# Turning two of the first four blocks by DMA and pairing the first loads in a four-layer attention and ReGLU kernel

## The chip, the cores and the metric

One NeuronCore of a Trainium2 chip. The metric is the device time of one execution in microseconds (us), taken on several executions; medians and ranges are quoted. Each run also carries the mean clock granted to TensorE (1.000 is full). Names: PE is TensorE, DVE is VectorE, ACT is ScalarE, SP is the SyncE queue that issues most DMAs. A second DMA queue is issued from ACT. PSUM holds the results of matmuls until another engine has read them. A DMA "lands" when its completion is signalled.

## The reference, cut to what matters

```python
x = x + A(layernorm(x), wqkv, wo)            # linear attention, 32 heads of 32
x = x + B(layernorm(x), Wg, Wu, Wd)          # (relu(x Wg) * (x Wu)) Wd
x = x + A(...)                               # the same two layers once more
x = x + B(...)
# in A:  q, k, v = x @ wqkv;  phi(t) = where(t > 0, t + 1, exp(t)) + 1e-6
```

x has 2048 rows of 1024, all inputs are bf16. The 2048 rows are 16 blocks of 128; four blocks are a "quarter". A matmul needs the normalized rows transposed, so every block must be "turned".

## The kernel before

The change and the argument touch the first 60 us alone: loads of x and of the weights, LayerNorm of the first blocks, and quarter 0 of layer 0. x0 to x15 are the blocks of x; k0, k1 and q0, q1 are the weights of the first and the last 512 columns of the keys and the queries, v0 the first of the values. A *unit* is one 128x512 tile of keys or queries: eight matmuls. `norm(n)` computes the LayerNorm statistics of block n and `scale(n)` applies them; what the *join* is stands in the code. Cuts are marked.

```python
zero = self.ep.tile([P, NW], BF16, tag="e")          # idle matmuls, to warm the PE clock
nc.vector.memset(zero, 0.0)
idle = self.ps3.tile([P, NW], F32, tag="b")
for _ in range(10):
    nc.tensor.matmul(idle, lhsT=zero[:, 0:P], rhs=zero, start=True, stop=True)
k0, k1, v0, q0, q1 = (ring.place() for _ in range(5))
self.load_x(0, 0, nc.scalar)       # first half of block 0, on ACT's queue
self.load_x(0, 1)                  # second half, on SP's
self.load_x(1, None, nc.scalar)
k0(0, H)                           # weights of the keys' first 512 columns, first half
self.load_x(2, None, nc.scalar)
k0(H, 2 * H)
self.load_x(3, None, nc.scalar)
k1(); q0()
self.load_x(4); ... ; self.load_x(7)
q1()
for t in range(8, self.ST): self.load_x(t)
v0()
...
def block(j, c, n):                # scale block n, turn it on PE, copy it out of PSUM on ACT
    scale(n)
    t0 = turn(n, 0); t1 = turn(n, 1)
    t0("s"); t1("s")
    if n + 1 < QT: norm(n + 1)
    k(j, c)
return [block0, block1, lambda: k(0, 1), lambda: block(1, 1, 2), lambda: k(2, 0),
        lambda: block(2, 1, 3), lambda: k(3, 0), lambda: k(3, 1)]      # then eight query units
...
def phi(self, ps, out, kind):      # ACT makes e; DVE's "join" reads PSUM and frees it
    ...
    def join():
        if kind == "v":            # keys: e = min(e, 1) + 1e-6
            nc.vector.tensor_scalar(out=e, in0=e, scalar1=1.0, scalar2=1e-6, ...)
        nc.vector.scalar_tensor_tensor(out=out, in0=ps, scalar=0.0, in1=e,
                                       op0=ALU.max, op1=ALU.add)
    if self.phi_lag: self.later.at(self.phi_lag, join)   # 3 units later in quarter 0
...
for i in range(QT, self.ST):       # LayerNorm of blocks 4 to 15, one every 3 units from unit 8
    self.ln_at((8 if l == 0 else 2) + 3 * (i - QT), l, i, 2)
```

Projections rotate through four PSUM buffers, so a unit cannot start before the join of the unit four places earlier has ended. In quarter 0 the order of instructions on DVE and ACT is the program's.

## Time and profile before

| | us |
|---|---|
| median of the first three runs (range) | 1629.38 (1629.17 to 1629.80) |
| the run whose trace was at hand for the prediction | 1630.68, span 1628.9 |
| PE busy in that trace | 1621.7 |
| PE idle before 11.56 us | 4.0 |
| second half of k0 lands | 10.19 |

A second trace of this unchanged kernel, taken in the experiments (a run of 1629.20 us), has this in its chain of waits (start, duration, what):

```profile
1.66 7.06 DMA t<-in_A_wqkv_dram
8.71 0.04 issue
8.76 0.59 PE ps L404 x2
```

The same load of k0, issued at the same 1.66 us, lands at 8.71 us in place of 10.19, and PE runs on 1.5 us sooner. The spans of the two traces are 1627.4 and 1628.9. On average over the first 8.7 us, the later trace moves 275 GB/s, 2.39 MB in all, and the first 261 GB/s, 2.27 MB. At the 360 GB/s that both reach, the difference is worth a third of a microsecond, so most of the 1.5 us seems to lie in which bytes came first, not in how many. All 41 later runs of this kernel fall into two groups with a gap between: 25 from 1629.12 to 1629.60, the other 16 from 1630.21 up. Two traces, one from each group, are all that ties the groups to this landing; and seven of the 16, but none of the 25, have a mean clock below 1.000, so the clock may have a part in it.

### The profile page before, as it was taken

What the parts mean: (1) busy time and instruction counts of PE and PEld (TensorE: products, weight loads), DVE (VectorE), ACT (ScalarE), POOL (GpSimd) and SP (SyncE); (2) the same over time, 40 slices, a digit from 0 to 9 for tenths busy, and PEclk for the clock granted to TensorE, in tenths of its full rate; (3) what the DMA queues carried; (4) which work ended last, traced back from release to release, by engine and by line L of the source; (5) the groups of instructions that cost most, each with busy time, mean ns of one, the idle gap of its engine ahead of it and who ended that gap; (6) DMA issues with size and microseconds to landing.
All of it is one profiled execution on the core that took longest, in us unless ns stands there. A gap on an engine that the chain in (4) does not pass through costs nothing.

```text
span 1628.9 us, 18772 instructions
## 1 busy us (share of the span) xinstructions
PE 1621.7 (100%) x7754; PEld 739.3 (45%) x7754; DVE 566.7 (35%) x940; ACT 331.8 (20%) x638; POOL 201.9 (12%) x134
## 2 busy tenths in 40 slices
PE   8999999999999999999999999999999999999999
PEld 4444444444444444444444444444444444444444
DVE  7845695213212222212165547942022111111211
ACT  5741212101110110111066312121011101101110
POOL 2349220000000000000023592100000000000000
DMA  7312647448445444544560147464554454454452
GB/s 245 65 52 56 178 71 206 144 148 232 155 143 190 160 151 161 168 147 137 168 128 1 53 93 250 85 193 146 182 165 152 155 184 155 145 166 154 155 162 71
DMA packets 298246, 235.06 MB, mean 144 GB/s; under 512 B 101296, under 2 KB 294192, under 8 KB 298160
## 3 DMA queue, kind: packets, MB, share of 16 engines
q1 hardware_dynamic: 292832, 228.75, 47.7%
q10 hardware_dynamic: 5328, 5.11, 0.9%
q8 instruction: 60, 0.98, 0.3%
q14 instruction: 26, 0.21, 0.0%
HBM read 201.33 MB, written 8.39 MB: 129 GB/s over the span
## 4 chain that ended last, share of the span: by engine, by line
PE 98%; ACT 1%; DVE 1%; DMA 1%; issue 0%; SPq 0%; DVEq 0%
PE pu L639 24%; PE pg L639 24%; PE acc L663 23%; PE ps L404 12%; PE ps L530 7%; PE ps L439 7%; DMA t<-in_A_wqkv_dram 1%; PE kv L452 0%; PE acc_last L663 0%; ACT e L351 0%; ACT e L350 0%; PE fold L515 0%; DVE st L138 0%; ACT e L352 0%; DVE slab L358 0%
## 5 line engine op out<-in xcount | busy, mean ns | idle before, releaser
L639 PEld LDWEIGHTS <-t 128*128 128x128 bf16 x3584 | 350.3, 98 | 423.2
L639 PE MATMUL pu<-xnT,t 128*128 128x512 bf16 x1792 | 423.5, 379 | 0.0
L639 PE MATMUL pg<-xnT,t 128*128 128x512 bf16 x1792 | 423.4, 379 | 0.0
L663 PE MATMUL acc<-t,hT 128*128 128x512 bf16 x1764 | 382.5, 379 | 0.0
L645 DVE TENSOR_TENSOR hT<-pu,rg 128x512 bf16<-128x512 f32 x224 | 154.7, 691 | 572.0 <-PE pu L639 572.0
L644 ACT ACTIVATE rg<-pg 128x512 f32<-128x512 f32 x224 | 133.5, 596 | 737.3 <-PE pg L639 737.0
L663 PEld LDWEIGHTS <-hT 128*128 128x128 bf16 x1820 | 177.9, 98 | 209.1
L404 PE MATMUL ps<-t,xnT 128*128 128x512 bf16 x1024 | 224.3, 380 | 2.2 <-DMA t<-in_A_wqkv_dram 1.7
L404 PEld LDWEIGHTS <-xnT 128*128 128x128 bf16 x1024 | 99.2, 98 | 122.3 <-issue 4.3
L530 PE MATMUL ps<-T,pqT 128*128 128x512 bf16 x512 | 111.2, 379 | 0.0
L145 ACT ACTIVATE rstd<-mv,eps 128x1 f32<-128x1 f32 x64 | 18.7, 293 | 334.1 <-DVE mv L143 333.9
L680 DVE TENSOR_TENSOR xo<-x,acc 128x512 bf16<-128x512 f32 x31 | 21.3, 688 | 170.3 <-PE acc L663 170.3
L483 POOL TENSOR_TENSOR prod<-pq,zrow 128x1024 f32<-128x1024 bf16 x32 | 67.9, 2122 | 85.9 <-DVE den L488 72.5
L138 DVE BATCH_NORM_STATS2 stats<-x 128x6 f32<-128x512 f32 (+1 forms) x120 | 78.0, 673 | 0.8
L530 PEld LDWEIGHTS <-pqT 128*128 128x128 bf16 x512 | 49.9, 98 | 60.4 <-issue 0.5
L419 POOL CAST ksum<-x 128x512 f32<-128x512 bf16 x2 | 1.7, 866 | 605.4 <-DVE x L358 605.4
L677 DVE TENSOR_TENSOR x<-x,acc 128x512 f32<-128x512 f32 x32 | 21.6, 675 | 138.5 <-PE acc L663 137.4
L421 POOL TENSOR_TENSOR ksum<-ksum,slab 128x512 f32<-128x512 f32 x46 | 54.0, 1183 | 84.6 <-DVE slab L358 75.1
L358 DVE SCALAR_TENSOR_TENSOR pq<-ps,e 128x512 bf16<-128x512 f32 x64 | 44.0, 688 | 53.9 <-ACT e L352 52.2
L495 POOL TENSOR_TENSOR pq<-pq,den 128x1024 bf16<-128x1024 bf16 x32 | 61.7, 1933 | 3.1 <-DVE den L490 3.1
L488 DVE TENSOR_REDUCE den<-prod 128x32 f32<-128x1024 f32 x32 | 39.0, 1217 | 53.9 <-POOL prod L483 53.9
L439 PE MATMUL ps<-slab,x 128*128 128x512 bf16 x256 | 56.6, 379 | 0.0
(57 smaller groups left out, 596.0 us busy)
## 6 DMA issues: line engine op xcount, KB each, us to landing
t<-in_B_W_gate_dram SPq DMA_DIRECT2D x56, 1024.0 KB, 7.1
t<-in_B_W_up_dram SPq DMA_DIRECT2D x56, 1024.0 KB, 5.4
t<-in_B_W_down_dram SPq DMA_DIRECT2D x64, 896.0 KB, 5.2
t<-in_A_wqkv_dram SPq DMA_DIRECT2D x11, 1024.0 KB, 5.6
t<-in_A_wo_dram SPq DMA_DIRECT2D x4, 1024.0 KB, 7.2
away<-x SPq DMA_DIRECT2D x8, 512.0 KB, 4.4
x<-away SPq DMA_DIRECT2D x8, 512.0 KB, 8.5
out_dram<-xo ACTq DMA_DIRECT2D x31, 128.0 KB, 2.5
```

Of the source, the lines that this page charges most:

```text
L138: self.nc.vector.bn_stats(out=stats[:, c, :], in_=src[:, c * fmax:(c + 1) * fmax])
L358: nc.vector.scalar_tensor_tensor(out=out, in0=ps, scalar=0.0, in1=e, op0=ALU.max, op1=ALU.add)
L404: nc.tensor.matmul(by_row(ps), lhsT=self.xnT[l, l_q][:, kt, j * P:(j + 1) * P], rhs=w[:, kt, :].rearrange("p (b i d) -> p i b d", i=R, d=H ...
L421: nc.gpsimd.tensor_tensor(out=ksum[:, cols], in0=ksum[:, cols], in1=pk, op=ALU.add)
L439: nc.tensor.matmul(ps, lhsT=self.xn[l, t][:, d * P:(d + 1) * P], rhs=self.pk[l, t][:, h * NW:(h + 1) * NW], start=(t == 0), stop=(t == sel ...
L483: nc.gpsimd.tensor_tensor(out=prod, in0=pq_of[sc, j], in1=zrow, op=ALU.mult)
L495: nc.gpsimd.tensor_tensor(out=heads(pq), in0=heads(pq), in1=den[:, :].unsqueeze(2).to_broadcast([P, D // HD, HD]), op=ALU.mult)
L530: nc.tensor.matmul(ps, lhsT=pqT[sc][:, g, j * P:(j + 1) * P], rhs=T[g // 2][:, g % 2, n2 * NW:(n2 + 1) * NW], start=(g == 0), stop=(g == G ...
L639: nc.tensor.matmul(ps, lhsT=w[:, kt, fi * P:(fi + 1) * P], rhs=self.xnT[l, q][:, kt, :], start=(kt == 0), stop=(kt == KT - 1))
L644: nc.scalar.activation(out=rg, in_=pg, func=ACT.Relu)
L645: nc.vector.tensor_tensor(out=h[:, fi, :], in0=pu, in1=rg, op=ALU.mult)
L663: nc.tensor.matmul(ps[:, 0:n], lhsT=hT[ft // 4][:, ft % 4, j * P:(j + 1) * P], rhs=wd[:, k, i * n:(i + 1) * n], start=(ft == 0), stop=(ft ...
```

## The change

Blocks 2 and 3 are turned by DMA transposes in place of PE transposes, and query units are put among the key units to give those transposes time. The first loads go out in pairs, one on each queue; x4 and later are issued behind the transposes. Two more idle matmuls.

```diff
-        for _ in range(10):
+        for _ in range(12):
...
-        self.load_x(0, 0, nc.scalar)
-        self.load_x(0, 1)
-        self.load_x(1, None, nc.scalar)
-        k0(0, H)
-        self.load_x(2, None, nc.scalar)
-        k0(H, 2 * H)
-        self.load_x(3, None, nc.scalar)
-        k1()
-        q0()
-        (x4 to x7, q1, x8 to x15, v0, all on SP's queue)
+        self.load_x(0, None, act)
+        self.load_x(1)
+        k0(H, 2 * H, act)
+        k0(0, H)
+        self.load_x(2, None, act)
+        k1()
+        q0(0, 2 * H, act)
+        self.load_x(3)
+
+        def load():
+            for t in range(4, 8):
+                self.load_x(t)
+            q1()
+            for t in range(8, self.ST):
+                self.later.at(3 + (t - 8) // 2 * 2, lambda t=t: self.load_x(t))
+            self.later.at(11, v0)
...
-        def block(j, c, n): ...
+        def turned(n):
+            scale(n)
+            self.ln_turn(0, n, xn[n])              # DMA transpose
+        return ([block0, block1, lambda: (turned(2), norm(3), k(0, 1)),
+                 lambda: (turned(3), load(), k(1, 1)), lambda: q(0, 0), lambda: q(1, 0)]
+                + [lambda f=f, j=j, c=c: f(j, c) for j in (2, 3) for f, c in ((k, 0), (k, 1), (q, 0))]
+                + [lambda j=j: q(j, 1) for j in range(QT)])
...                                                # SP too now keeps the program's order
```

More of the change, by code (lines that the diff above doesn't have):

```diff
@@ L34, in place @@
         self.loaded += 1
-        return lambda lo=0, hi=8: self.nc.sync.dma_start(out=t[:, lo:hi, :], in_=src[:, lo:hi, :])
+        return lambda lo=0, hi=8, queue=None: (queue or self.nc.sync).dma_start(
+            out=t[:, lo:hi, :], in_=src[:, lo:hi, :])
     def load_to(self, n):
@@ L218, in head @@
         idle = self.ps3.tile([P, NW], F32, tag="b")
-        for _ in range(10):
+        for _ in range(12):
             nc.tensor.matmul(idle, lhsT=zero[:, 0:P], rhs=zero, start=True, stop=True)
         k0, k1, v0, q0, q1 = (ring.place() for _ in range(5))
-        self.load_x(0, 0, nc.scalar)
-        self.load_x(0, 1)
-        self.load_x(1, None, nc.scalar)
+        act = nc.scalar
+        self.load_x(0, None, act)
+        self.load_x(1)
+        k0(H, 2 * H, act)
         k0(0, H)
-        self.load_x(2, None, nc.scalar)
-        k0(H, 2 * H)
-        self.load_x(3, None, nc.scalar)
-        k1()
-        q0()
-        self.load_x(4)
-        self.load_x(5)
-        self.load_x(6)
-        self.load_x(7)
-        q1()
-        for t in range(8, self.ST):
-            self.load_x(t)
-        v0()
+        self.load_x(2, None, act)
+        k1()
+        q0(0, 2 * H, act)
[7 more added lines that the diff above has]
+            self.later.at(11, v0)
         src = self.xb
@@ L269, in turn, with head_units @@
             return take
-        return stat, rstd, scale, turn
-    def head_units(self, k, stat, rstd, scale, turn):
+        return load, xn, stat, rstd, scale, turn
+    def head_units(self, k, q, load, xn, stat, rstd, scale, turn):
         def block0():
@@ L305, in norm @@
             rstd(j)
-        def block(j, c, n):
+        def turned(n):
             scale(n)
-            t0 = turn(n, 0)
-            t1 = turn(n, 1)
-            t0("s")
-            t1("s")
-            if n + 1 < QT:
-                norm(n + 1)
-            k(j, c)
-        return [block0, block1, lambda: k(0, 1), lambda: block(1, 1, 2), lambda: k(2, 0),
-                lambda: block(2, 1, 3), lambda: k(3, 0), lambda: k(3, 1)]
+            self.ln_turn(0, n, xn[n])
[3 more added lines that the diff above has]
+                + [lambda j=j: q(j, 1) for j in range(QT)])
     def ln_turn(self, layer, t, xn):
@@ L562, in layer_A @@
         if l == 0:
-            first = self.head_units(lambda *a: k_unit(0, *a), *steps)
+            first = self.head_units(lambda *a: k_unit(0, *a), lambda *a: q_unit(0, *a), *steps)
         else:
@@ L569, in quarter0 @@
             run(first)
-            run(column_major(q_unit, 0))
-            later.at(1, lambda: None)
             self.phi_lag = 0
         if l == 0:
-            with self.tc.manual_schedule(engines={mybir.EngineType.DVE,
+            with self.tc.manual_schedule(engines={mybir.EngineType.DVE, mybir.EngineType.SP,
                                                   mybir.EngineType.Activation}):
```

## The prediction

> **What bounds the kernel now.** I read the page first: its busy times and its chain of waits.
>
> ```profile
> PE 1621.7 (100%) x7754; PEld 739.3 (45%) x7754; DVE 566.7 (35%) x940; ACT 331.8 (20%) x638; POOL 201.9 (12%) x134
> ...
> PE 98%; ACT 1%; DVE 1%; DMA 1%; issue 0%; SPq 0%; DVEq 0%
> ```
>
> TensorE (PE) is busy for 1621.7 of 1628.9 us, so all idle time together is 7.2 us, under half a percent. The change touches only the loads, the first LayerNorms and the first quarter of layer 0. A comparison of the two instruction streams per engine says the same: past this first stretch they are equal in order. So the question is at which microsecond PE leaves the first quarter. Busy time by stretch shows where PE is idle:
>
> ```profile
> core 0: us, PE busy (x) PEld busy (x) DVE busy (x) ACT busy (x) POOL busy (x), PEclk, DMA share, GB/s
> 0.00:11.56 11.56, 7.54 (x34) 3.02 (x35) 5.54 (x16) 2.92 (x7) 0.70 (x6) 1.00 0.85 285
> 11.56:19.90 8.34, 8.26 (x52) 3.96 (x50) 7.85 (x16) 4.75 (x12) 2.80 (x3) 1.00 1.08 362
> 19.90:38.90 19.00, 19.00 (x90) 8.61 (x88) 15.66 (x31) 14.72 (x29) 5.79 (x5) 1.00 0.69 194
> 38.90:60.00 21.10, 20.98 (x97) 9.34 (x96) 20.81 (x43) 16.68 (x41) 5.11 (x5) 1.00 0.46 75
> ```
>
> PE loses 4.0 us before 11.56, and 0.08, 0.00 and 0.12 us in the next three rows. The other 3 us lie in the tail, which is untouched. From 11.56 us on the DMA share is above 1 (362 GB/s): the DMA engines are full while PE works. VectorE (DVE) is nearly full in the row before PE's first transposes of block 3 and again after 38.9.
>
> The chain in order of time says what ends the 4 us and what paces the start (start, duration, what; lines left out):
>
> ```profile
> 1.66 8.53 DMA t<-in_A_wqkv_dram
> ...
> 10.23 0.59 PE ps L404 x2
> ...
> 14.98 1.28 DVE L138 BATCH_NORM_STATS2 st<-x 128x6 f32<-128x512 bf16 x2
> 16.30 0.21 DVE L143 BATCH_NORM_AGGREGATE mv<-st 128x2 f32<-128x12 f32 x1
> 16.42 0.37 DVE L356 TENSOR_SCALAR e<-e 128x512 f32<-128x512 f32 x1
> 16.90 0.69 DVE L358 SCALAR_TENSOR_TENSOR slab<-ps,e 128x512 bf16<-128x512 f32 x1
> ...
> 15.13 0.61 PE L260 MATMUL tp<-ident,x 128*128 128x128 bf16 x8
> 15.58 3.62 PE L404 MATMUL ps<-t,xnT 128*128 128x512 bf16 x16
> 19.28 0.62 PE L260 MATMUL tp<-ident,x 128*128 128x128 bf16 x8
> 19.90 6.92 PE ps L404 x32
> ```
>
> (The first two and the last line are of the chain; the others of the timeline, where a DVE or a PE line begins with its start and duration.) The second half of weight k0 lands at 10.19 us and starts PE for good. Then 32 matmuls take 6.92 us: 0.216 us each, 1.73 us for a unit of eight.
>
> **What the Trainium skill says.** "DMA: Bandwidth & Descriptors", section "Issuing engines are not separate DMA queues": loads from several issuing engines run on the same 16 DMA engines, and a second queue saves only issue time. The trace agrees: 346 GB/s from 5 to 10 us with two queues at work, 366 from 15 to 20 with one; an issue costs 0.4 to 0.5 us. So pairing changes the order of landing, not the total. "TensorE: Matmul & The Clock Gate", section "Part 4: PE-mode transpose", gives about 275 ns for a PE transpose in one kernel's context. Here eight start at 15.13 and the next matmul starts at 15.58, so one costs 56 ns of PE; the measurement decides. Same page, section "What's actually happening": the array needs about 3.4 us of sustained work to reach full clock. The trace agrees: ten idle matmuls take 4.45 us, twice the later 216 ns each. No page told me how long one DMA transpose takes; the trace does, 3.0 to 4.1 us from issue to landing for 128x1024.
>
> **The change part by part.**
>
> *PE transposes.* Sixteen go (blocks 2 and 3). By the timeline, 11.56 to 19.74 us holds 32 matmuls (6.90 us) and sixteen transposes: 8.18 us, so transposes with their small waits cost 1.28 us (0.90 of it the transposes). Saved if nothing takes their place: 1.3 us. ScalarE loses four PSUM copies of 0.54 us, off the path. Two more idle matmuls fill the wait for x0; they end at about 6.6 us and cost nothing.
>
> *The start.* Time to landing, issue by issue, before: x0 3.6 and 3.75 us, x1 5.2, k0 first half 5.7, x2 9.3, k0 second half 10.2, x3 10.5, k1 13.4, q0 16.4. Now x0 and x1 come side by side, then the two halves of k0, 1.5 MB in all. The DMA moved that many bytes by 6.9 us, and landings trail bytes moved by 1 to 2 us, so k0 is there at about 8.4 instead of 10.2. x0 comes about 0.7 us later than before, which puts the first real matmul at 8.2 to 8.4. Idle time saved: about 1.7 us at best.
>
> *What is now late: k1.* It shares the queues with x2 and then q0. At equal shares it ends when 3.7 MB are through: about 15. If q0 gets little until k1 is done, 12.8. PE wants it at 8.4 plus two units, 3.9 us with block 1's transposes, so 12.3. A wait of 0.5 to 2.8 us.
>
> *What is now late: x3.* It moves from the third x load on ScalarE's queue (landed 10.5) to behind k1 on SP's. The first 4.2 MB (x0 to x3, k0, k1, q0) are the same set of bytes in both kernels; before, the last landed at 16.4. Now x3 and q0 end that set, so x3 lands at about 15.5 to 16.4, at the earliest 14 if SP's queue gets the larger share.
>
> *And DVE waits for it in order.* In the changed program's DVE order the statistics of x3 stand ahead of the first join of the keys (lines "e" and "slab" above). There are four PSUM buffers, so the fifth unit, q(0,0), cannot start before that join ends. From the rows above: statistics 1.28, aggregate 0.21, join 0.37 + 0.69, with gaps 2.61 us (14.98 to 17.59 in the old trace). So q(0,0) starts at x3 plus 2.6: 18.1 to 19.0, 16.8 with the early x3 (there k1 at 13.3 and two units set it too).
>
> *The balance.* After q(0,0) starts, twelve units remain, 20.7 us, without PE transposes. The old kernel has eleven units after 19.90, so it ends the quarter at 38.9 and stood twelve units from the end at 18.2. The change is then 18.1 - 18.2 = -0.1 to 19.0 - 18.2 = +0.8 us, -1.4 in the best case. The gain of 1.7 + 1.3 us at the start is thus eaten by one load. The later waits: keys and queries are mixed in the second half, so ScalarE (a query takes 0.58 + 0.63 + 0.72 us, more than PE's 1.73 with the gaps) falls less behind than with eight queries in a row. The 0.12 us of PE idle near 44 us may go, but DVE enters 38.9 to 60, where it was busy for 20.81 of 21.10, with up to 1 us more backlog. I count -0.1 to +0.5.
>
> *DMA transposes.* Block 2's is wanted at about 22 (q(0,0) plus two units), issued at about 13.3 and behind x3 in the queue: lands by 18 or 19. Block 3's is issued at about 19.5, lands by 23.5, wanted at about 27. Both hidden. x4 can only be issued after it, about 20.5, and lands at about 23; q1 at about 28, wanted at about 32. Hidden too.
>
> **Rivals.** (1) *The start's gain stays.* If pairing equal loads keeps the 16 DMA engines even (landings trailed bytes by 2 us only once two unequal streams had mixed), x3 lands at 14 to 15 and the kernel gains 1 to 1.5 us: 1628. For it: k1 and q0 need only the same bytes. Against it: no view shows that pairing evens them. (2) *x3 at the end of the set holds DVE and PE*: 1629.3 to 1630.5, my main line. For it: the program's order and the equal set of bytes. (3) *Mixed queues trail further*: landings slip from 2 to 3 or 4 us behind, x3 at 17.5, and the late x4 to x7 push the normalizations into the full DVE stretch: 1631 to 1632. Against it: the trail stayed at 2 us once established. (4) *PE is the bound, all is hidden anyway* and only the transposes count: 1628. Against it: PE is not busy in the start, loads set it.
>
> **Range and chances.** Main line +0.2, with some weight on the first rival because the two queues look arranged to be even, gives 1629.4 us against 1629.38. Best case -1.5, worst about +2: the range is 1627.8 to 1631.2. Two per cent is 33 us, over four times all of PE's idle time, and a loss of that size would need a stall that nothing in the order suggests. Same: 0.98.
>
> **What would show it.** Right: first matmul of layer 0 before 9 us; in the waits, PE waiting for k1 near 12 to 15 and for DVE's join before the fifth unit; DVE idle for 2 to 3 us until x3; no PE wait on a DMA transpose; PE leaving the quarter within 1 us of the old time. Wrong: x3 landing before 14, with PE continuous from 9 us (gain of 2 us or more), or waits on transposes, x4 to x7 or q1, or new PE idle time between 40 and 60 us (loss).

## The result, and the profile after

| | runs | median us | range |
|---|---|---|---|
| before | 4 | 1629.30 | 1629.17 to 1629.80 |
| changed | 4 | 1631.49 | 1629.61 to 1632.99 |

A ratio here is the mean time of one kernel's runs over that of the other's of the same rounds, so not quite the ratio of the medians. It is 1.0012, 95% interval 0.9995 to 1.003: the same at two per cent, as forecast, but the median lies 0.3 us above my range. The spread is new too: four runs cover 3.4 us. In order, with their clocks: 1629.61 (1.000), 1631.14 (0.999), 1632.99 (0.998), 1631.85 (0.999). The trace at hand is of the first, the fastest. Its busy times by stretch, in the windows used before:

```profile
0.00:11.56 11.56, 9.23 (x41) 3.83 (x42) 6.33 (x18) 3.47 (x7) 0.70 (x6) 1.00 0.87 284
11.56:19.90 8.34, 7.50 (x35) 3.05 (x33) 6.95 (x15) 3.67 (x9) 1.84 (x2) 1.00 0.71 175
19.90:38.90 19.00, 19.00 (x90) 8.63 (x89) 18.14 (x34) 15.21 (x32) 4.71 (x5) 1.00 1.08 297
38.90:60.00 21.10, 20.91 (x98) 9.41 (x97) 21.10 (x45) 16.91 (x40) 8.27 (x7) 1.00 0.43 82
```

The columns are stretch, length, busy time of PE, PE weight loads, DVE, ACT, POOL, granted clock, DMA share and GB/s. PE is busy for 1.7 us more before 11.56, half of which (0.85) is the two idle matmuls, and for 0.8 less in the next row. The DMA share fell from 1.08 to 0.71 there: x4, issued at 5.75 us before, is now issued at 18.52, behind the transposes. DVE is full in the last row. PE's own timeline and its list of waits name the losses:

```profile
1.34 5.30 PE L221 MATMUL idle<-zero 128*128 128x512 bf16 x12 [1.34 <-DVE zero L218]
7.26 0.72 PE L262 MATMUL tp<-ident,x 128*128 128x128 bf16 x8 [0.62 <-DVE x L155]
8.35 1.47 PE L402 MATMUL ps<-t,xnT 128*128 128x512 bf16 x6 [0.37 <-ACT xnT L269]
...
10.56 1.90 PE L402 MATMUL ps<-t,xnT 128*128 128x512 bf16 x8
13.13 7.13 PE L402 MATMUL ps<-t,xnT 128*128 128x512 bf16 x30 [0.67 <-DMA t<-in_A_wqkv_dram]
```

x0 landed at 4.6 us, so the first real matmul came at 8.35, and k1 landed at 13.09, after PE had run dry. The third wait is the forecast one on DVE's order. On DVE and on PE's weight loads:

```profile
14.21 1.28 DVE L139 BATCH_NORM_STATS2 st<-x 128x6 f32<-128x512 bf16 x2 [0.47 <-DMA x<-in_A_x_dram]
15.53 0.21 DVE L144 BATCH_NORM_AGGREGATE mv<-st 128x2 f32<-128x12 f32 x1
15.66 0.37 DVE L354 TENSOR_SCALAR e<-e 128x512 f32<-128x512 f32 x1
...
16.07 0.69 DVE L356 SCALAR_TENSOR_TENSOR slab<-ps,e 128x512 bf16<-128x512 f32 x1
...
16.81 1.62 PEld L402 LDWEIGHTS <-xnT 128*128 128x128 bf16 x9 [0.56 <-DVE slab L356]
```

DVE idles for 0.47 us until x3 lands at 14.19, does its statistics, then the first join, and the fifth unit starts at 16.81: x3 plus 2.6 us, as worked out beforehand. No wait on a DMA transpose appears anywhere. From the first matmul of layer B on (237.47 us here, 238.48 in the first trace before) the two traces take 1390.36 and 1390.42 us to the end, so all of the difference lies ahead of that.

### The profile page after: what moved, and what is told of

Same layout as the page of the kernel before. It is cut to its first block, busy times and chain, and to the rows that moved or that the text cites. A ratio compares the mean times of both kernels' runs of the same rounds, so it can differ in the third digit from the quotient of the medians.

```text
span 1627.8 us, 18743 instructions
## 1 busy us (share of the span) xinstructions
PE 1621.6 (100%) x7740; PEld 739.5 (45%) x7740; DVE 567.6 (35%) x940; ACT 330.5 (20%) x634; POOL 202.0 (12%) x134
## 4 chain that ended last, share of the span: by engine, by line
PE 98%; DMA 1%; DVE 1%; issue 0%; SPq 0%; DVEq 0%
PE pu L635 24%; PE pg L635 24%; PE acc L659 23%; PE ps L402 13%; PE ps L528 7%; PE ps L437 7%; DMA x<-in_A_x_dram 1%; PE kv L450 0%; PE acc_last L659 0%; PE fold L513 0%; DVE slab L356 0%; DVE stats L139 0%; DVE e L354 0%; DVE st L139 0%; DVE pq L356 0%
## 5 line engine op out<-in xcount | busy, mean ns | idle before, releaser
L419 POOL TENSOR_TENSOR ksum<-ksum,slab 128x512 f32<-128x512 f32 x46 | 54.1, 1183 | 81.4 <-DVE slab L356 64.1
L486 DVE TENSOR_REDUCE den<-prod 128x32 f32<-128x1024 f32 x32 | 38.9, 1217 | 54.0 <-POOL prod L481 54.0
```

What stands on the lines that cost most here:

```text
L419: nc.gpsimd.tensor_tensor(out=ksum[:, cols], in0=ksum[:, cols], in1=pk, op=ALU.add)
```

## The experiments

Fourteen runs, each with five rounds. "Half" counts the runs whose mean clock was below 1.000.

| label | what | median us (range) | half |
|---|---|---|---|
| e1 | before, unchanged | 1629.39 (1629.20 to 1632.28) | 1 of 5 |
| e2 | changed, unchanged | 1630.29 (1630.17 to 1631.59) | 1 of 5 |
| e3 | changed, 10 idle matmuls | 1631.15 (1630.82 to 1632.59) | 5 of 5 |
| e4 | changed, 16 idle matmuls | 1630.71 (1629.80 to 1630.99) | 0 of 5 |
| e5 | changed, x0 in halves | 1631.01 (1630.29 to 1631.68) | 2 of 5 |
| e6 | changed, join first | 1631.43 (1630.36 to 1632.73) | 3 of 5 |
| e7 | old first loads, DMA transposes | 1628.92 (1628.71 to 1629.27) | 0 of 5 |
| e8 | new loads, PE transposes | 1631.97 (1630.54 to 1632.57) | 4 of 5 |
| e9 | e7 with join first | 1629.85 (1629.34 to 1630.10) | 0 of 5 |
| e10 | e9, LayerNorm 1 unit later | 1629.02 (1628.73 to 1629.09) | 0 of 5 |
| e11 | e4 with join first | 1630.55 (1630.46 to 1631.22) | 0 of 5 |
| e12 | e7, LayerNorm 1 unit later | 1628.90 (1628.87 to 1629.48) | 0 of 5 |
| e13 | e7, LayerNorm 2 units later | 1628.38 (1628.33 to 1628.53) | 0 of 5 |
| e14 | e4, LayerNorm 1 unit later | 1630.22 (1629.93 to 1630.43) | 0 of 5 |

The kernel before, in the same rounds: median 1630.21 beside e1 to e4, 1629.59 beside e5 to e8, 1629.47 beside e9 to e11, 1629.41 beside e12 to e14, nine runs each. Every interval of a ratio contains 1, and all results were correct. The four groups (e1 to e4, e5 to e8, e9 to e11, e12 to e14) ran on four chips. The fastest run of the kernel before was 1629.12, 1629.25, 1629.12 and 1629.19 on them, so I compare across groups, but only differences well over 0.1 us.

Not all forecasts below came in. Inside a range that was named are the medians of e3, e11 and e12 (its less hopeful case); e10 and e14 missed theirs by 0.02 us. Outside all that was named lie e4 (0.7 us above, though its clocks came as forecast), e7 (0.3 above), e9 (0.75 above), e13 (0.5 faster than e12, forecast was the same or a loss), and e5, whose three runs at full clock have a median of 1630.84. e6 and e8 are spoiled by the clock.

### Clock or noise: e1 to e4

e1 and e2 are the two kernels again. e3 and e4 change one number of the changed kernel:

```diff
-        for _ in range(12):
+        for _ in range(10):      # e3;  range(16) in e4
```

> The kernel before, unchanged, for a second trace. Theory A (the changed kernel's runs differ by how long the TensorE clock stays at half rate): every run of the kernel before has a mean granted clock of 1.000 and lies within 1629.0 to 1630.7; the profiled run of 1630.68 differs from 1629.3 by a later landing of the second half of k0 (10.2 us there, about 9 here). Theory B (chip or run noise): this one spreads over 2 us or more as the changed kernel does.

> The changed kernel, unchanged, for more draws and another trace. Theory A: times in steps of about 1.7 us (one activity window of 3.4 us at half rate costs half of it): 1629.6, 1631.3, 1633.0, each with mean clock 1.000, 0.999, 0.998. Theory B: no link of time to clock.

> The changed kernel with 10 idle matmuls as before in place of 12. If fewer idle matmuls leave PE less busy in the first microseconds, half rate lasts longer or comes more often: median 1631 to 1633. If the count does not matter (the gaps for k1 and the join do), the same spread as the changed kernel.

> The changed kernel with 16 idle matmuls: they end at 7.3 us or, cold, at 8.2, which fills the gap before the transposes of block 0. Theory A with the warm-up as cause: all runs at clock 1.000, median 1629.5 to 1630. If half rate comes from the later gaps (0.7 us for k1, 0.2 us for the join), the spread of 1629.6 to 1633 stays.

With nine runs of the changed kernel in hand (four at first, five in e2): five at full clock, 1629.61 to 1630.35; four below it, 1631.14 to 1632.99. The means differ by 1.75 us. e3 is below full clock in all five runs, e4 in none. The trace of e3 shows how it comes about (columns as above; the clock comes last but two):

```profile
1.34:4.50 3.16, 3.15 (x8) 1.20 (x9) 0.00 (x0) 0.68 (x1) 0.00 (x0) 1.00 0.80 185
4.50:7.90 3.40, 0.72 (x4) 0.10 (x1) 2.04 (x4) 0.47 (x2) 0.00 (x0) 1.00 1.08 370
7.90:11.33 3.43, 2.64 (x12) 1.34 (x13) 2.69 (x8) 1.02 (x4) 0.00 (x0) 0.50 1.09 355
11.33:14.74 3.41, 3.41 (x15) 1.73 (x14) 0.95 (x3) 0.60 (x1) 0.00 (x0) 0.50 0.93 308
14.74:18.15 3.41, 3.41 (x17) 1.56 (x16) 2.78 (x6) 0.98 (x3) 0.00 (x0) 1.00 0.07 25
```

PE's timeline of the same run has the gap (in brackets: idle before, and who ended it):

```profile
8.43 1.04 PE L262 MATMUL tp<-ident,x 128*128 128x128 bf16 x8 [3.21 <-DVE x L155]
9.73 2.74 PE L402 MATMUL ps<-t,xnT 128*128 128x512 bf16 x6 [0.26 <-ACT xnT L269]
```

The clock records of this trace begin at 4.50 us, and PEclk reads 1.00 where there is no record. The idle matmuls tell what it was before: they start 0.43 us apart until 4.50 and 0.22 us apart after it, so the clock came up there. Then PE stood for 3.21 us, until the late x0 was normalized: 0.72 us busy in 3.40. From 7.92 to 14.74 us the granted clock is 0.50, and the real matmuls that fall into this stretch take twice as long: six end after 2.74 us where the changed kernel's first trace has 1.47. The Trainium skill says in "TensorE: Matmul & The Clock Gate", section "What's actually happening", that the clock's state follows the activity in free-running windows of 3413 ns; the clock records agree. From 4.50 to 7.92 it is one such length and from 7.92 to 14.74 two; in e5, e6 and e8 the half-rate stretch is one, 3.41 us. Where the window lies differs from run to run: with idle matmuls that all start at 1.34 us, the clock comes up at 4.04 us in e6, 6.69 in the changed kernel's first trace and 7.29 in that of e2. What PE does in the 3.41 us after that is what tells the traces apart: 0.72 to 1.38 us of work in the four that then fall to half rate (e3, e6, e8, e5), 1.94 to 2.75 us in the eight others that have clock records. That is an agreement of twelve traces, and only the count of idle matmuls was varied on purpose.

So Theory A held for the changed kernel, where every run below full clock is slower than every run at it, and Theory B fell there. e1 was a miss for Theory A: it spread over 3.1 us, the very sign named for B. Its longest run, though, is again one of low clock (1632.28 at 0.998): the kernel before can lose its clock too (7 of 41 in all), only less often. e4 removes the half-rate runs but not the loss: with the clock full it is still at 1630.7. Its trace starts as that of e2 does (the third unit at 13.84 us in both) and loses 0.45 us more between 38.9 and 60 us (PE busy for 20.57 against 21.02), where DVE is full. The clock explains the upper part of the spread, not all of the change.

### Which load: e5; old loads with the rest of the change: e7; new loads with PE transposes: e8

```diff
 e5
-        self.load_x(0, None, act)
-        self.load_x(1)
+        self.load_x(0, 0, act)
+        self.load_x(0, 1)
+        self.load_x(1)
 e7   (first loads of the kernel before; load() and the DMA transposes stay)
-        self.load_x(0, None, act); self.load_x(1); k0(H, 2 * H, act); k0(0, H)
-        self.load_x(2, None, act); k1(); q0(0, 2 * H, act); self.load_x(3)
+        self.load_x(0, 0, act); self.load_x(0, 1); self.load_x(1, None, act)
+        k0(0, H); self.load_x(2, None, act); k0(H, 2 * H); self.load_x(3, None, act)
+        k1(); q0()
 e8   (loads of the change; block() of before turns blocks 2 and 3, units in its order)
-            self.ln_turn(0, n, xn[n])
+            t0 = turn(n, 0); t1 = turn(n, 1); t0("s"); t1("s")
+            norm(n + 1) if n + 1 < QT else load()
```

> The changed kernel with x0 again in two halves, one on each queue, x1 after it. Theory C (the late x0 costs the gain: it landed at 4.4 to 5.6 us in place of 3.6 to 3.8, and the PE gap before its transposes lets the clock fall to half rate): x0 lands by 3.9, first real matmul at about 7.5, clock 1.000 in all runs, median 1628.8 to 1629.6. Rival D (k1 and the join of the first keys set the end of the quarter whatever comes before): first matmul earlier, but the waits for k1 and the join grow by as much, time 1629.6 to 1630.4 where the clock is full.

> The first loads as before the change (x0 in halves, x1 to x3 on ScalarE's queue, k0, k1, q0 on SP's), with blocks 2 and 3 turned by DMA and the later loads as in the changed kernel. My sum: first matmul at 7.5 us, continuous from the landing of the second half of k0 (8.7 or 10.2 us), then 27.2 us to the end of the quarter, 1.3 us less than the kernel before from the same landing: median 1628.0 to 1628.6, 1629.3 where k0 lands late. If the DMA transposes or x4 to x7 behind them bring new waits: 1629.5 or more.

> The new loads with blocks 2 and 3 turned by PE and the units in the old order: what the loads alone do. PE transposes and their waits cost 1.3 us; x3 is needed before its unit k(2,1) at about 17 us and then has 2.6 us of DVE work ahead. Expected 1.3 us slower than the changed kernel at full clock: 1630.9 to 1631.6; half-rate runs as often as there. If loads alone are faster than before: under 1629.2.

e5: x0 landed at 3.7 us, as in the kernel before, and nothing was won. One half of k0 landed at 9.2 and k1 at 14.5; PE waited 2.2 us for that half of k0 where it had waited for x0, so the first real matmul came at 9.25, not at 7.5, and two of five runs still lost their clock. Theory C, that x0 alone is to blame, fell. Its rival D is right that nothing is won, but not in the way that it gave: the wait moved to k0, not to k1 and the join. In this trace, what x0 gained on the changed kernel's first trace k0 lost (9.2 for 8.5 us) and k1 too (14.5 for 13.1).

e7 shows the way out: all five runs at 1628.71 to 1629.27, full clock in all, where the changed kernel's full-clock runs had 1629.61 to 1630.35. Only the first loads differ between the two. Against the kernel before, e7 is not the transposes alone: the new order of units, the later x4 to x15 and the two idle matmuls are in it too. The old order of loads is a staggered one. These lines of the two traces (DMA issues: what, queue, count, KB, median us from issue to landing, each from a narrow window at its issue time) are of the changed kernel first, then of the second trace before, whose order of first loads e7 has. In the first fence the lines are x1, x0 and k1, in the second the halves of x0 and k1:

```profile
x<-in_A_x_dram SPq DMA_DIRECT2D x1, 256.0 KB, 3.7
x<-in_A_x_dram ACTq DMA_DIRECT2D x1, 256.0 KB, 3.9
...
t<-in_A_wqkv_dram SPq DMA_DIRECT2D x1, 1024.0 KB, 11.4
```

```profile
x<-in_A_x_dram SPq DMA_DIRECT2D x1, 128.0 KB, 2.8
x<-in_A_x_dram ACTq DMA_DIRECT2D x1, 128.0 KB, 2.9
...
t<-in_A_wqkv_dram SPq DMA_DIRECT2D x1, 1024.0 KB, 9.5
```

In e7, x0 lands at 3.6, k0 at 8.9, k1 at 11.8, x3 at 9.0 and q0 at 14.7. In the changed kernel x0 lands at 4.6, k0 at 8.5, k1 at 13.1, x3 at 14.2 and q0 at 14.8. The set of 4.2 MB ends at the same time in these two traces; between traces of one order it differs more (16.4 in the first trace before, 15.6 in that of e2). On one queue, one behind the other, k1 and q0 land 2.9 us apart; on two queues side by side, 1.7 apart, and it is k1 that moves, while q0 is wanted only two units, 3.5 us, after it.

e8 was to show the loads alone. Four of its five runs lost the clock; the one at full clock, 1630.54, is no basis. Among half-rate runs it has a mean of 1632.14 against 1631.89 for the changed kernel. Nor is it the loads alone: with no DMA transpose in SP's queue, x4 is issued at 5.29 us, for 18.52 in the changed kernel, and q0 lands at 17.05. I leave it as inconclusive.

### DVE's order and DVE's backlog: e6, e9, e11, then e10, e12 to e14

```diff
 e6, e9, e11   (statistics of x3 after the first join of the keys)
-        lambda: (turned(2), norm(3), k(0, 1)),
-        lambda: (turned(3), load(), k(1, 1)),
+        lambda: (turned(2), k(0, 1)),
+        lambda: (norm(3), turned(3), load(), k(1, 1)),
 e10, e12, e14 (one unit later; 10 in e13)
-        self.ln_at((8 if l == 0 else 2) + 3 * (i - QT), l, i, 2)
+        self.ln_at((9 if l == 0 else 2) + 3 * (i - QT), l, i, 2)
```

> The changed kernel with the statistics of x3 moved behind the first join of the keys in DVE's order. The wait of PE for the join (0.2 to 0.5 us) goes. If that wait ended last, 0.2 to 0.5 us are gained in runs of full clock (1629.3 to 1629.9); if k1 sets the pace behind it, nothing. Half-rate runs as often as in the changed kernel (4 of 9).

> The old first loads, blocks 2 and 3 by DMA, and the statistics of x3 behind the first join of the keys. In the trace with old loads alone PE lost 0.5 us at 15.2 before the fifth unit and 0.25 us at 17.5. If DVE's order causes both, they go: median 1628.2 to 1628.5 (1628.92 without). If DVE is simply full there, they come back at the next buffers: 1628.7 to 1629.1.

> The changed kernel with 16 idle matmuls and the statistics of x3 behind the first join, to see the join's wait at full clock. Clock 1.000 in all runs. If the join's wait ended last, 0.2 to 0.5 us less than with 16 idle matmuls alone (1630.71): 1630.2 to 1630.5. If k1 and DVE's load set the pace: 1630.5 to 1630.9.

> As the one before, with the normalizations of x4 to x15 one unit later. PE lost 0.7 us at 52.4 in the trace with old loads, where DVE is busy for 21.10 of 21.10 us. If DVE's backlog from the first quarter causes that wait, moving the normalizations changes it by some tenths, either way; if the total is unchanged, another wait takes its place. Expected 1628.2 to 1629.0.

e6 was spoiled by the clock (three of five). e11 asks the same at full clock: 1630.55 against 1630.71 for e4, less than the spread. With the old loads, e9 even costs 0.9 us (1629.85 against 1628.92, and no run of the one reaches those of the other). The wait for the first join, which I had forecast and which is plainly in the trace, can be removed without gain: in e7's trace PE stands for 0.5 us before the fifth unit and 0.25 before the sixth, in e9's not before the fifth but for 0.9 us before the sixth. What e10 won back on e9 is seen in the row for 38.9 to 60 us; e9, then e10, then the best version, e13:

```profile
38.90:60.00 21.10, 20.25 (x94) 9.05 (x93) 21.10 (x45) 16.37 (x38) 8.26 (x7) 1.00 0.42 79
```

```profile
38.90:60.00 21.10, 20.98 (x98) 9.37 (x96) 21.04 (x43) 16.26 (x39) 8.78 (x7) 1.00 0.40 75
```

```profile
38.90:60.00 21.10, 21.10 (x99) 9.59 (x98) 20.86 (x44) 17.20 (x39) 9.01 (x7) 1.00 0.40 75
```

The first figure after the comma is PE's busy time: 20.25, 20.98, 21.10. DVE's is 21.10, 21.04, 20.86. Only the normalizations of the later blocks moved from e9 to e10, by one unit, and PE got back 0.73 us, the run 0.83. e9's loss against e7 stands in this row only in part (20.25 against 20.57). My reading: with DVE full, a normalization that comes early holds up the joins that free PSUM buffers for PE. In e9's trace PE loses 0.5 us at 39.6 and 0.7 us at 54.1, up to 40 us after the code that e9 changed, in e10's 0.1 at 42.4 and 0.3 at 56.5.

> Old first loads, blocks 2 and 3 by DMA, statistics of x3 where the change has them, normalizations of x4 to x15 one unit later. If DVE's backlog cost 0.5 to 0.8 us at 39 to 60 us: median 1628.1 to 1628.5 (1628.92 without). If the wait only moves: 1628.8 to 1629.0.

> As before it, two units later. If one unit was enough: the same within 0.2 us. If the transposes of x4 then come too late for the second quarter (wanted at about 37 us): a wait on a DMA transpose and 1629 or more.

> The changed kernel with 16 idle matmuls (full clock) and normalizations one unit later. If DVE's backlog is what is left of the loss: 0.5 to 0.8 us faster than with 16 idle matmuls alone (1630.71), 1629.9 to 1630.2, PE busy for 20.9 or more of 21.1 us between 38.9 and 60. If the late start sets it: 1630.5 to 1630.9.

e12, one unit later without the moved join, changes nothing on e7 in the median (1628.90 against 1628.92), so the hopeful case was missed. Trace against trace it does: PE is busy for 20.98 of the 21.10 us, 20.57 in e7's trace, which is of e7's slowest run (1629.27). In e12's trace the first real matmul comes at 8.12 us, 7.74 in that of e7, and 0.12 us of PE idle time are left at 56 us. How often e7's other runs had the later wait is not known. e13, two units later, takes 0.5 us off: five runs within 0.2 us at 1628.33 to 1628.53, all below each of the nine runs of the kernel before of the same rounds (1629.19 to 1630.88). Its ratio to before is 0.9991, 95% interval 0.9979 to 1.0004. That is 1.0 us on the medians and the best version found. e14 answers the last question: with full clock and a later LayerNorm the changed kernel stands at 1630.22 against 1630.71, so the backlog was about 0.5 us of e4's loss (PE's busy time in 38.9 to 60 us: 20.57 in e4, 20.98 in e14). In e2's trace, at 21.02, there was less of it to win. About 0.8 us against the median of before of the same rounds (1629.41) is left, and its trace has k1's wait (0.6 us) and the late first matmul (8.70 us), as e4's has (9.11).

### The sum at full clock

Compare the second trace before (1629.20 us) with the trace of e2 (1630.17). First before, then e2:

```profile
7.46 1.04 PE L404 MATMUL ps<-t,xnT 128*128 128x512 bf16 x4 [0.36 <-ACT xnT L267]
...
10.09 3.63 PE L404 MATMUL ps<-t,xnT 128*128 128x512 bf16 x16
```

```profile
9.08 1.47 PE L402 MATMUL ps<-t,xnT 128*128 128x512 bf16 x6 [0.36 <-ACT xnT L269]
...
11.30 1.90 PE L402 MATMUL ps<-t,xnT 128*128 128x512 bf16 x8
13.84 8.40 PE L402 MATMUL ps<-t,xnT 128*128 128x512 bf16 x36 [0.64 <-DMA t<-in_A_wqkv_dram]
```

The third unit starts at 11.8 us (10.09 plus one unit of 1.73) and at 13.84: 2.0 us later in the changed kernel, from the late first matmul (9.08 against 7.46, partly made good because k0 is then there) and from k1. From there to the first matmul of layer B it is 225.2 and 224.2 us: 1.0 us less. That is what the DMA transposes with the new order of units bring, after the new waits. 2.0 lost, 1.0 won, and spans of 1627.4 and 1628.4 us. With the changed kernel's first and fastest trace in place of e2's it is 1.3 lost (13.13) and 0.9 won, and a span of 1627.8.

## Why the prediction was right or wrong

- **Same within two per cent, with the changed kernel near the one before:** right. **The range 1627.8 to 1631.2:** missed by 0.3 us in the rounds that counted; five more rounds gave 1630.29. The five runs at full clock (1629.61 to 1630.35) lie inside it; the four others reach from 1631.14 to 1632.99. The main line, +0.2 us or 1629.4, is below all nine.
- **"PE bound, all change in the first 60 us, the rest equal":** right; 1390.4 us from layer B on in both traces.
- **PE transposes, 1.3 us saved:** about right. 0.9 to 1.0 us was measured net of the new waits.
- **"The start ... Idle time saved: about 1.7 us at best": this step failed.** The 1.7 us was the wait for k0, which landed at 10.2 in a trace of a run of 1630.68 us, and I added the balance to a median of 1629.38. The typical run has k0 at about 8.7 (by its one trace) and only 0.25 us to save. Against that the start is 1.3 to 2.0 us later, not 1.7 earlier. Even in the trace that I read the term was too large. The second unit started at 10.56 for 11.56, 1.0 us earlier: the 1.7 leaves out the late x0 of the same paragraph, and half of the idle time saved went to idle matmuls. The balance itself has the same fault in its "stood twelve units from the end at 18.2". In the second trace before, everything after the landing comes 1.5 us sooner, so that point is 16.7. With q(0,0) measured at 16.8 (first trace) and 17.5 (e2), the same balance then gives +0.1 and +0.8; by the first matmul of layer B it was +0.5 and +1.0. The mechanism of the balance held; its zero was wrong.
- **"x0 comes about 0.7 us later":** 0.9 us in the fastest trace, 1.6 in e2, 2.1 in e3. The term had the right sign and was too small.
- **"Two more idle matmuls ... cost nothing": this step failed too, by what it left out.** I quoted the warm-up, but did not ask what clock PE keeps while it waits for the late x0. Nor is the warm-up a fixed 3.4 us: in the traces with paired loads the clock came up 2.7 us (e6) to 5.9 us (e2) after the first idle matmul. Four of nine runs were at half rate for a while and 1.75 us slower on average; the count of idle matmuls alone moves that from five of five to none of five. None of my four rivals had it. The late x0 makes the gap and the clock makes it cost: this puts the median of the first rounds above the range.
- **k1 late, wait of 0.5 to 2.8 us:** right, 0.6 to 0.7 us. **x3 at 15.5 to 16.4:** earlier, 14.2 to 14.9 in the changed kernel's two traces, near the early case. **q(0,0) at x3 plus 2.6:** right to 0.1 us. But what it costs was mis-read: moving the join ahead won nothing in e11 and lost in e9.
- **"DVE enters 38.9 to 60 with up to 1 us more backlog; -0.1 to +0.5":** right in place, and 0.5 us by e14 against e4; in the changed kernel's own two traces PE is idle there for 0.19 and 0.08 us, 0.12 in both traces before.
- **Rival 1, that pairing evens the queues and x3 lands early:** half of it came. x3 landed at 14.2, but the gain did not. **Rival 3 and PE waits on transposes, x4 to x7 or q1:** not seen. Blocks 2 and 3 landed at 16.9 and 20.3 us, before the 18 to 19 and the 23.5 that were forecast.
- **The signs:** the waits for k1 and for the join came. The first matmul came before 9 us in the first trace (8.35) and just after in e2 (9.08). "DVE idle for 2 to 3 us until x3" did not come: 0.47 us, as x3 landed early.

Open: what sets the two groups of the kernel before, beyond the two traces and the clock; and why x0's landing differs by 1.2 us between runs of the paired order.

## What to carry to other kernels

When a sum of tenths is built on one trace, check first where the run of that trace lies among the others, and add the sum to that run, not to the median. When the first loads keep the DMA engines full, order them by when each is wanted; here, with x0 beside x1 and k1 beside q0, x0 landed 0.9 to 2.1 us later and k1 1.3 us or more. And ask of every new idle stretch of TensorE near the start how it changes the clock: 16 idle matmuls, which shorten the wait, kept the clock full in all fifteen runs that had them, even where they did not make the time shorter.

## What the Trainium skill lacked or had wrong

- "TensorE: Matmul & The Clock Gate", section "What's actually happening", puts the ramp's penalty under 1% of a typical span and advises not to fit a specific count of slow matmuls. True of the size: half-rate runs of the changed kernel were 1.75 us, 0.1%, slower. But that is more than the 1 us by which the kernels differ, so here the count of idle matmuls mattered (with the paired loads, 10: five of five runs at half rate for a while; 16: none of fifteen). The section speaks of busy and idle windows, but not of how much work makes a window busy: in these traces 1.38 us of work in 3.41, or less, was followed by half rate, and 1.94 or more was not. The longest gap could be as short as 1.85 us (e8).
- Same page, "Part 4: PE-mode transpose": about 275 ns in one kernel's context. That section does not say what transposes in a row cost. Here one is recorded as 0.22 us long, but they overlap: eight 128x128 in a row cost 0.45 us of PE, 56 ns each.
- "DMA: Bandwidth & Descriptors", section "Issuing engines are not separate DMA queues", fits the sums (4.2 MB ended at 14.7 us from staggered and at 14.8 from paired queues in the faster trace of each), but says nothing on which load lands first: with a pair, k1 landed at 13.1 in place of 11.7 us. The nearest to it is the page's section "Queues, rings and completion order", where each engine takes turns between queues by packet; it has no landing times.
- "VectorE: DVE Perf Modes", section "The three transpose paths", which I had overlooked, gives 1309 ns for a DMA transpose of 128x128. No page has it for 128x1024 or behind loads: twelve of 128x1024 in the first trace took 3.0 to 4.7 us from issue to landing, 3.2 in the median; in the changed kernel two that were issued behind loads took 8.1 and 9.1.
